# Roots of a layer norm moved from VectorE to GpSimd, and a new order for all pieces of a Fourier-mixing and feed-forward kernel

## The chip, the cores and the metric

The kernel runs on one core of a Trainium2 chip. The metric is the device time of one execution in microseconds (us), as the median of several runs; less is better. The core has five engines with a queue of instructions each: PE (TensorE, matmuls), DVE (VectorE), ACT (ScalarE), POOL (GpSimd) and SP (SyncE, which here only issues transfers). Each works through its own queue in order, and waits at an instruction until the semaphores that it needs are set.

## The reference

The input `x` has 2048 rows of 512 numbers. The first half mixes the normed rows by a discrete Fourier transform along both axes and keeps the real part; the second is a feed-forward block with SiLU. Both add their input back.

```python
def _layernorm(x, axis=-1, eps=1e-5):
    m = jnp.mean(x, axis=axis, keepdims=True)
    v = jnp.var(x, axis=axis, keepdims=True)
    return (x - m) / jnp.sqrt(v + eps)
...
    a = jnp.einsum("bsd,ed->bse", x, dft_hid_re)
    b = jnp.einsum("bsd,ed->bse", x, dft_hid_im)
    y = jnp.einsum("ts,bse->bte", dft_seq_re, a) - jnp.einsum("ts,bse->bte", dft_seq_im, b)
...
    h = jnp.einsum("bsd,df->bsf", x, w1)        # w1: 512 x 1792
    out = jnp.einsum("bsf,fd->bsd", _silu(h), w2)
...
    h = x + _A_ref(_layernorm(x, axis=-1), ...)
    h2 = h + _B_ref(_layernorm(h, axis=-1), B_w1, B_w2)
```

All is in 32-bit floats. The change concerns the second norm, that of `h`.

## The kernel before, in words

**The products.** Each matrix product is split into blocks of two by two, and seven block products (numbered 1 to 7 in the code) replace the eight. Each factor is split into a rounded part and its remainder (`ph` and `pl`, `gth` and `gtl`, `wah` and `wal`, ...): ACT writes the rounded part (`rounded`, L301), DVE the remainder (L305 or L307), and a product takes three matmuls, high by high, high by low and low by high (`three`, `mul_add`, L364). So each piece of data passes ACT and then DVE before PE can use it.

**The stages** run in this order on PE: `plain` and `fast` (the transform along the rows, tiles `raw` from `in_seq`, accumulated as `c` and `m`), `mix_fast(0)` (the transform along the columns, `y`, which gives `h` for one half of the 2048 positions, q = 0), then `fast` twice and `mix_fast(1)` for the other half, q = 1; then `up(0)` (first feed-forward product), `down(0)` (second), `up(1)` and `down(1)`. In `up`, a bank `y` holds one block product; ACT seeds a second bank `vx` from it (L1127), reads finished banks into tiles `g` with SiLU (L1113) or as a copy (L1116), and DVE adds a bank to `g` (L1119).

**The accumulating loads.** In `fast`, one of the operands of product 4 is made by a transfer: POOL issues a load that adds to a tile already in memory (`prep(4, jj)`, L783, `raw<-in_seq` on POOL). It can only be issued when product 6 no longer needs the tile (its remainder, L307, is the last reader), and must land before ACT and DVE can round it for product 4.

**The norm of h** is done by `norm_h`, once for each q and each half `tau`: four times. Rows of `h` lie along the partitions' direction here, so sums run over the partitions: `total` (L951 to L953) adds tiles on DVE and then reduces over all partitions on POOL (`partition_all_reduce`). The steps are: mean (`m`), centering (`hr`, L970), squares (`sq`, ACT, L974), variance (`v`), `row` (L980: POOL writes one row of sums to memory, `tk<-v`), `gather` (L985: POOL reads it back as 128 x 4, `rs<-tk`), `root` (L988 and `guess`) and `finish` (`steps`), both on DVE: they make 1/sqrt by an integer guess and three Newton steps, 12 instructions of 128 x 4; then POOL writes the result (L994, `tk<-rs`) and `spread` reads it to all partitions (L997, `v<-tk`), DVE scales `hr` (L1001) and POOL stores it (`nd<-hr`, L1006). `up` loads it later as `hn`.

**What sets the order.** Each piece (a function that issues a few instructions) gets a time when `program` builds its list: the time of the matmuls that need it, less a lead. A table `MOVED` adds a number of us to almost every one of these times, by the piece's number, and the pieces are issued in the order of the sums:

```python
    return sorted(((t + MOVED.get(n, 0.0), at, n, f) for t, at, n, f in events), key=lambda v: v[:3])
```

`fnet_ffn_kernel` ties the instructions of each engine to this order. The numbers mean nothing else: no time is waited for.

Of the kernel before, what the change touches and what calls it, by code (L numbers as in the profile page):

```python
# [10 lines left out]
I32 = mybir.dt.int32  # L11
# [37 lines left out]
    0: -293.31, 1: -238.02, 2: -236.08, 3: -179.9, 4: -165.03, 5: -165.94, 6: -230.19, 7: -165.91, 8: -166.37, 9:  # L49
    -169.09, 10: -87.55, 11: -75.38, 12: -79.62, 13: -88.41, 14: -92.69, 15: -95.8, 16: -82.48, 19: -265.67, 20:  # L50
    -161.2, 21: -158.27, 22: -323.002, 23: -165.782, 24: -160.652, 26: -268.028, 27: -160.838, 28: -143.038, 30:
    -169.334, 31: -135.774, 32: -99.584, 33: -268.444, 34: -162.004, 35: -86.794, 36: -89.044, 37: -319.344, 38:
    -134.664, 39: -53.134, 40: -18.294, 41: -135.054, 42: -110.964, 44: -173.98, 45: -89.04, 46: -19.29, 48:
    -180.186, 49: -98.766, 50: -24.876, 52: -185.652, 53: -171.502, 54: -73.442, 56: 0.292, 57: -19.018, 58: 0.252,
    59: -274.468, 60: -148.358, 61: -33.588, 62: 8.892, 63: -181.978, 64: -103.138, 65: -34.758, 66: -2.358, 67:
    -66.878, 68: -27.768, 69: -25.578, 71: -43.566, 72: -38.236, 73: -59.346, 74: -38.886, 75: 10.024, 76: 1.064,
    78: -16.394, 79: -14.734, 80: -26.784, 81: -5.694, 82: -0.564, 84: -41.482, 85: -36.432, 86: -157.702, 87:
    -22.612, 88: -7.752, 89: -7.192, 91: -2.708, 92: -3.74, 93: -2.72, 94: -64.5, 95: -32.87, 96: 1.73, 97: 0.63,
    98: -27.44, 99: -34.19, 100: -7.38, 101: 0.97, 102: -18.82, 103: -15.52, 104: -11.25, 106: -2.098, 107: -14.178,
    108: -61.718, 109: -48.848, 110: -158.978, 111: -50.148, 112: -26.248, 114: 1.066, 115: 2.704, 116: 7.464, 118:  # L60
    -9.124, 119: -1.244, 121: -6.812, 122: -8.972, 123: -6.6, 125: 1.36, 126: -14.5, 127: -11.28, 129: 4.452, 130:
    0.362, 131: 6.052, 132: -3.788, 133: -5.948, 135: -7.456, 136: -8.176, 138: 6.046, 139: -21.664, 140: -11.904,
    142: -1.932, 143: -0.232, 145: 1.25, 146: -25.88, 147: -6.3, 148: 21.31, 149: -4.7, 150: -20.4, 151: -8.98, 152:
    -7.15, 153: 28.75, 154: 25.81, 155: -12.71, 156: 17.2, 157: 14.33, 158: 24.01, 159: 24.3, 160: -25.07, 161:
    -19.07, 162: -1.94, 163: -9.48, 164: -10.03, 165: -0.79, 166: -3.22, 167: -4.24, 168: -0.47, 169: -1.31, 170:
    -20.28, 171: -13.2, 172: -9.02, 173: -7.06, 174: -8.33, 175: 7.5, 176: 2.08, 177: 4.54, 178: 4.16, 179: 7.35,
    180: -87.56, 181: -39.38, 182: -35.83, 183: -51.3, 184: -49.53, 185: -33.05, 186: -38.96, 187: -40.12, 188: -33,
    189: -7.63, 190: -7.07, 191: -7.39, 192: -28.2, 193: -21.42, 194: -12.55, 195: -45.58, 196: -38.52, 197: -25.77,
    198: -18.72, 199: -6.37, 200: 1.76, 201: -8.06, 202: -8.83, 203: 0.74, 204: -13.44, 205: -35.74, 206: -14.86,
    207: -15.13, 208: -14.61, 209: -14.99, 210: -11.05, 211: -13.19, 212: -1.42, 213: -6.67, 214: 2.44, 215: 3.39,  # L70
    216: 2.15, 217: 13.71, 218: 15.04, 219: -19.36, 220: -15.08, 221: -8.75, 222: -16.8, 223: -12.74, 224: -12.69,
    225: -2.55, 226: 1.87, 227: 7.08, 228: -24.27, 229: 4.79, 230: 6.22, 232: -11.018, 233: -2.838, 234: 4.432, 236:
    -5.006, 237: -3.076, 238: -0.206, 240: -7.874, 241: 1.516, 242: -0.314, 244: 2.218, 245: -10.572, 246: -7.142,
    247: 3.998, 249: 2.16, 250: 3.43, 251: 1.34, 253: 1.272, 254: 9.412, 255: 7.882, 257: -20.866, 258: -2.706, 259:
    1.564, 261: 8.456, 262: 3.496, 263: 4.736, 264: 5.326, 266: 1.238, 267: 4.798, 268: 3.258, 270: -3.49, 271: 2.1,
    272: 7.94, 274: 4.282, 275: 3.402, 276: 5.252, 278: 3.804, 279: 4.694, 280: 6.494, 281: -2.616, 282: -2.776,
    283: -1.126, 284: -6.436, 286: 2.026, 287: 5.116, 289: -8.752, 290: -0.782, 292: 7.54, 293: 5.47, 294: 6.35,
    295: 8.38, 296: 7.83, 297: 0.87, 299: 4.962, 300: 4.012, 301: 6.532, 303: -3.486, 304: 0.024, 306: 1.046, 307:
    -0.484, 309: 1.838, 310: 4.768, 311: 3.708, 312: 2.558, 313: 1.518, 314: -1.802, 316: 0.69, 317: 5.59, 318:
    2.19, 320: 3.402, 321: 5.322, 323: 4.884, 324: 4.194, 326: 4.326, 327: 4.666, 328: 6.196, 329: 5.956, 330:  # L80
    6.206, 331: -3.854, 333: 3.888, 334: 5.218, 335: 3.598, 336: 6.828, 338: -2.26, 339: 1.69, 341: -0.06, 342:
    -4.778, 343: -2.228, 345: 2.484, 346: 5.364, 347: 5.104, 348: 10.804, 350: 3.936, 351: -23.884, 352: -20.924,
    353: -3.474, 354: -1.064, 355: -3.958, 356: -1.394, 357: 1.542, 358: 4.454, 359: -1.334, 360: -4.352, 361:
    -1.014, 362: 0.566, 363: -7.054, 365: -0.542, 366: -0.194, 367: 0.208, 369: -1.59, 370: -0.702, 371: 2.89, 372:
    -1.892, 374: 3.672, 375: 3.862, 376: -7.108, 378: 5.504, 379: 11.454, 380: 0.624, 381: 3.244, 382: -7.318, 384:
    5.186, 385: 5.316, 386: -4.694, 388: 0.178, 389: 6.128, 390: 7.108, 391: 4.988, 392: -4.022, 394: -3.05, 395:
    0.01, 396: 0.91, 398: 2.112, 399: 5.002, 400: 4.232, 401: -3.148, 403: 3.004, 404: 7.374, 405: -13.516, 407:
    -2.874, 408: 0.456, 409: 6.836, 410: 4.696, 411: -1.684, 413: -2.082, 414: 2.008, 415: -4.502, 417: 4.08, 418:
    11.49, 419: 1.48, 420: -0.59, 421: 0.25, 423: -1.248, 424: -3.288, 425: -2.488, 427: 6.394, 428: 6.564, 429:
    16.874, 430: -13.816, 431: -15.286, 432: -16.006, 433: -16.926, 434: -18.866, 435: -13.776, 436: -14.006, 437:  # L90
    -14.416, 438: -11.876, 439: -2.636, 440: 5.724, 441: 4.534, 442: -2.046, 443: 4.424, 444: -32.796, 445: -23.056,
    446: -33.396, 447: -25.156, 448: -20.266, 449: -17.146, 450: -18.596, 451: -10.076, 452: -14.966, 453: -16.196,
    454: -8.346, 455: -8.386, 456: -15.576, 457: 7.224, 458: -31.606, 459: -1.696, 460: -0.956, 462: 11.206, 463:
    7.706, 464: 7.99, 466: -1.482, 467: -3.772, 468: 2.778, 470: 2.2, 471: 6.07, 472: 5.6, 474: 5.262, 475: -6.768,
    476: 7.382, 477: 5.232, 479: -3.576, 480: 4.644, 481: 2.494, 483: 1.896, 484: 1.986, 485: 7.656, 487: -32.282,
    488: -0.712, 489: -2.882, 491: 10.11, 492: 5.77, 493: 7.89, 494: 6.92, 496: 1.662, 497: 6.492, 498: 5.412, 500:
    3.054, 501: 2.056, 502: 2.074, 504: 13.106, 505: 6.506, 506: 4.726, 508: -0.03, 509: -0.312, 510: -2.412, 511:
    -11.742, 512: 0.03, 513: -1.16, 514: -12.122, 516: -2.98, 517: 0.14, 519: -2.788, 520: -4.408, 522: 1.934, 523:
    0.184, 524: -4.466, 525: -2.436, 526: -0.846, 527: -1.086, 529: 3.666, 530: 3.496, 531: -0.814, 533: -1.692,
    534: -1.132, 536: 3.25, 537: 3.27, 539: 7.492, 540: 5.312, 541: 0.362, 542: 2.642, 543: 8.322, 544: 1.364, 546:  # L100
    7.504, 547: 5.364, 548: 6.754, 550: -3.354, 551: 0.166, 553: 2.108, 554: 3.918, 556: 3.74, 557: 2.83, 558: 3.97,
    559: 2.9, 560: 2.21, 561: 1.07, 563: 2.202, 564: 2.302, 565: 2.142, 566: 8.252, 568: -5.946, 569: 0.184, 571:
    -0.01, 572: 6.046, 573: 4.706, 575: 7.928, 576: 4.098, 577: 1.978, 578: 5.368, 580: 16.1, 581: -43.508, 582:
    8.75, 583: 22.1, 584: 0.32, 585: 7.64, 586: 2.056, 587: 1.89, 589: -3.098, 590: -7.808, 591: -3.528, 593:
    -3.066, 594: -2.026, 595: 1.884, 597: 1.186, 598: -1.804, 599: -1.514, 601: 5.168, 602: 3.658, 603: 7.348, 604:
    7.838, 606: 9.74, 607: 4.81, 608: 5.2, 610: -46.978, 611: 9.892, 612: 7.782, 614: -4.116, 615: -2.096, 616:
    5.034, 618: 8.296, 619: 1.676, 620: 4.576, 621: 5.266, 623: -14.632, 624: 1.758, 625: 2.508, 627: 6.85, 628:
    4.44, 629: 5.41, 631: -3.658, 632: 1.672, 633: 3.992, 635: 3.514, 636: -6.306, 637: -5.556, 638: -26.046, 639:
    -27.206, 640: -24.446, 641: -25.296, 643: -9.124, 644: -6.024, 646: 2.478, 647: 1.388, 649: 1.76, 650: 3.11,
# [1330 lines left out]
```

## Time and profile before

| | us |
|---|---|
| median of 3 timed runs | 647.86 |
| the three runs | 647.58, 647.86, 649.74 |
| the profiled execution | 645.56 |
| its span, from the first to the last instruction | 643.8 |

In rows of the profile a time is counted from the start of the span. In a row of a timeline stand start, length, engine, line, operation, written tile `<-` read tiles, their shapes and a count `x2`; in brackets the idle time of the engine ahead of it and what ended it. In a row of groups stand the busy time and the mean in ns, then the idle time ahead of the instructions of the group. Rows with PEq, POOLq or SPq are those of an engine's sequencer or queue of transfers. Matmuls overlap: each row is longer than the time to the next one.

### The profile page before, as it was taken

The page shows a single profiled execution, that of the slowest core. Times are in us where ns is not written, and L with a number is a line of the kernel's source. Part 1 is how long each engine was busy: PE and PEld are TensorE (multiplying, and loading weights), DVE is VectorE, ACT ScalarE, POOL GpSimd, SP SyncE. Part 2 cuts the span into 40 slices and gives each one's busy share as a digit, 9 for nine tenths or more (in the row PEclk, how much of TensorE's full clock was granted, in tenths as well). Part 3 has the DMA queues.
Part 4 walks back from the last instruction along what each step waited for, and adds up shares of the span by engine and source line. Part 5 has one row for each costly group of instructions (what it writes and reads, how often), then busy time and mean ns, then how long its engine had stood idle before and what let it go on. Part 6 is the DMA issues. An engine that isn't in the chain of part 4 may idle for free. (4 is left out here: it accounts for less than half of the span.)

```text
span 643.8 us, 8291 instructions
## 1 busy us (share of the span) xinstructions
PE 631.3 (98%) x2892; PEld 543.9 (84%) x2892; DVE 562.2 (87%) x700; ACT 375.8 (58%) x484; POOL 110.1 (17%) x139
## 2 busy tenths in 40 slices
PE   9999999999999999999999999999999999999996
PEld 6888888888888888888888878877888888888885
DVE  7999999998978999999999999988989864479974
ACT  6898456765546545455855753779445555664700
POOL 0021111223103431310220027243010000000000
PEclk9999999999999999999999999999999999999999
DMA  9976899999999786999999899959998845278903
GB/s 317 369 184 147 261 358 377 302 322 358 330 306 350 242 263 154 367 361 331 333 352 396 281 295 373 382 207 328 362 369 287 297 147 177 82 261 309 344 33 131
DMA packets 59706, 184.22 MB, mean 286 GB/s; under 512 B 6800, under 2 KB 13840, under 8 KB 59664
## 3 DMA queue, kind: packets, MB, share of 16 engines
q1 hardware_dynamic: 43872, 127.03, 54.4%
q0 software_dynamic: 15504, 56.39, 29.1%
q8 instruction: 23, 0.38, 0.2%
q10 hardware_dynamic: 288, 0.26, 0.1%
q14 instruction: 19, 0.16, 0.1%
HBM read 139.34 MB, written 44.32 MB: 285 GB/s over the span
## 5 line engine op out<-in xcount | busy, mean ns | idle before, releaser
L301 ACT ACTIVATE ph<-raw 128x1024 fp32r<-128x1024 f32 x102 | 104.3, 1050 | 87.4 <-DMA raw<-in_seq 30.8
L364 PE MATMUL m<-ph,S 128*128 128x512 f32 x384 | 116.7, 379 | 0.0
L305 DVE TENSOR_TENSOR pl<-raw,ph 128x1024 fp32r<-128x1024 f32 x88 | 107.7, 1242 | 10.3 <-ACT ph L301 9.6
L364 PE MATMUL f<-gth,wf 128*128 128x512 f32 x322 | 98.1, 379 | 0.0
L364 PE MATMUL m<-ph,X 128*128 128x512 f32 x288 | 88.4, 379 | 0.0
L364 PEld LDWEIGHTS m<-ph,S 128*128 128x128 f32 x384 | 72.6, 189 | 10.2
L364 PE MATMUL m<-pl,S 128*128 128x512 f32 x192 | 72.9, 380 | 0.5 <-DVE pl L305 0.5
L364 PEld LDWEIGHTS f<-gth,wf 128*128 128x128 f32 x322 | 60.9, 189 | 8.8
L364 PE MATMUL y<-ph,hf 128*128 128x512 f32 x224 | 67.2, 379 | 0.3 <-DVE h L884 0.3
L364 PE MATMUL f<-gtl,wf 128*128 128x512 f32 x161 | 61.1, 380 | 0.0
L364 PEld LDWEIGHTS m<-ph,X 128*128 128x128 f32 x288 | 54.4, 189 | 7.6
L301 ACT ACTIVATE gth<-g 128x1024 fp32r<-128x1024 f32 x42 | 43.0, 1051 | 25.3 <-DVE g L1250 20.3
L364 PE MATMUL m<-pl,X 128*128 128x512 f32 x144 | 54.9, 381 | 0.2 <-DVE pl L305 0.2
L305 DVE TENSOR_TENSOR gtl<-g,gth 128x1024 fp32r<-128x1024 f32 x42 | 50.1, 1217 | 3.8 <-ACT gth L301 3.7
L364 PE MATMUL c<-ph,X 128*128 128x512 f32 x176 | 51.2, 381 | 0.5 <-DVE X L461 0.5
L364 PEld LDWEIGHTS y<-ph,hf 128*128 128x128 f32 x224 | 42.3, 189 | 6.6 <-issue 0.7
L769 DVE TENSOR_TENSOR raw<-raw,raw 128x1024 f32<-128x1024 f32 x36 | 45.8, 1274 | 2.1 <-DMA raw<-in_seq 1.7
L364 PE MATMUL y<-pl,hf 128*128 128x512 f32 x112 | 42.7, 381 | 1.2 <-DVE pl L305 1.2
L364 PEld LDWEIGHTS m<-pl,S 128*128 128x128 f32 x192 | 36.3, 189 | 6.0 <-DVE pl L305 0.9
L1119 DVE TENSOR_TENSOR g<-vx,g 128x512 f32<-128x512 f32 x28 | 19.3, 688 | 23.8 <-PE vx L364 12.0
L364 PEld LDWEIGHTS c<-ph,X 128*128 128x128 f32 x176 | 33.1, 189 | 6.0 <-DVE X L461 0.9
L364 PEld LDWEIGHTS f<-gtl,wf 128*128 128x128 f32 x161 | 30.4, 189 | 4.6 <-DVE gtl L305 0.3
(360 smaller groups left out, 1269.1 us busy)
## 6 DMA issues: line engine op xcount, KB each, us to landing
raw<-in_seq SPq DMA_DIRECT2D x84, 512.0 KB, 6.2
hf<-fd SPq DMA_DIRECT2D x28, 512.0 KB, 6.5
wf<-wd SPq DMA_DIRECT2D x28, 512.0 KB, 6.7
wf<-wd SPq DMA_DIRECT2D x28, 384.0 KB, 4.5
sf<-sd SPq DMA_DIRECT2D x18, 512.0 KB, 5.9
raw<-in_seq POOLq DMA_DIRECT2D x16, 512.0 KB, 6.8
fd<-hf POOLq DMA_DIRECT2D x14, 512.0 KB, 6.5
w<-in_ffn SPq DMA_DIRECT2D x23, 256.0 KB, 6.0
```

Source lines behind the costliest of these rows:

```text
L301: nc.scalar.activation(hi, src, AF.Copy, scale=sign)
L305: nc.vector.tensor_tensor(lo, src, hi, op=ALU.subtract)
L364: nc.tensor.matmul(acc, w, turned(m), **flags)
L769: nc.vector.tensor_tensor(o, a, b, op=ALU.subtract)
L1119: nc.vector.tensor_tensor(g[q, f][:, tau, :], src, g[q, f][:, tau, :], op=ALU.add)
```

## The change

**Roots on POOL.** `guess` and `steps` are gone. `root` now issues three instructions on GpSimd, one of them a power with exponent −0.5 (a tile `power` filled with it); `finish` issues four, one Newton step, and the transfer as before. The power and the reduction over partitions belong to different libraries of GpSimd, so a library change (a row `ISA` without tiles) stands ahead of the first root after a reduction, and of the first reduction after a root. A single power on one column is issued early, as a single reduction was before.

```diff
 MOVED = {
-    0: -293.31, 1: -238.02, 2: -236.08, 3: -179.9, 4: -165.03, 5: -165.94, 6: -230.19, 7: -165.91, 8: -166.37, 9:
...
+    power = keep.tile([P, 4], F32, name="power")
...
-    def guess(v, t, r, b):
-
-        nc.vector.tensor_scalar(r.bitcast(I32), v.bitcast(I32), -0.5, float(0x5F3759DF), op0=ALU.mult, op1=ALU.add)
-        newton(v, t, r, b)
-
-    def steps(v, t, r, b):
-        newton(v, t, b, r)
-        newton(v, t, r, b)
...
         def root():
-            nc.vector.tensor_scalar(ln["w"][0], ln["w"][0], 1.0 / D, EPS, op0=ALU.mult, op1=ALU.add)
-            nc.vector.tensor_scalar(ln["w"][1], ln["w"][0], -0.5, None, op0=ALU.mult)
-            guess(*ln["w"])
+            v, t, r, _ = ln["w"]
+            nc.gpsimd.tensor_scalar(v, v, 1.0 / D, EPS, op0=ALU.mult, op1=ALU.add)
+            nc.gpsimd.tensor_tensor(r, v, power, op=ALU.pow)
+            nc.gpsimd.tensor_scalar(t, v, -0.5, None, op0=ALU.mult)
 
         def finish():
-            steps(*ln["w"])
-            nc.gpsimd.dma_start(token[1].rearrange("(p j) -> p j", j=4), ln.pop("w")[3])
+            v, t, r, b = ln["w"]
+            nc.gpsimd.tensor_tensor(v, r, r, op=ALU.mult)
+            nc.gpsimd.tensor_tensor(v, v, t, op=ALU.mult)
+            nc.gpsimd.tensor_scalar(v, v, 1.5, None, op0=ALU.add)
+            nc.gpsimd.tensor_tensor(b, v, r, op=ALU.mult)
+            nc.gpsimd.dma_start(token[1].rearrange("(p j) -> p j", j=4), b)
...
+    nc.gpsimd.memset(power, -0.5)
     at(100, lambda: nc.scalar.activation(spare[:, :1], spare[:, 1:], AF.Silu))
+    at(105, lambda: nc.gpsimd.tensor_tensor(spare[:, :1], spare[:, 1:], power[:, :1], op=ALU.pow))
     at(110, lambda: nc.gpsimd.partition_all_reduce(spare[:, :1], spare[:, 1:], channels=P, reduce_op=REDUCE_ADD))
```

**A new order.** Nearly all entries of `MOVED` (1207 of 1208) have other numbers. PE's instructions keep their sequence; on DVE, ACT, POOL and SP pieces change places, by a few places mostly. DVE has 48 instructions fewer, POOL 37 rows more. Three places show it.

First, POOL during `fast(0, 1)`, the first transform stage for q = 1 (about 213 to 250 us of the span), from the first variance's row of sums to the transfers behind its root. `tk` and `rs` are the tokens of the norm, `m` the sums of the next mean, `raw` the accumulating loads, `cd` a store. Before:

```order
L980 DMA tk_82<-v_1972 16x1x32
L783 DMA raw_1855<-in_seq 128x1024
L985 DMA rs_2062<-tk_82 128x4
L953 ISA m_2097<-m_2097 128x512
L505 DMA cd_73<-c_2106 128x1024
L783 DMA raw_2009<-in_seq 128x1024
L994 DMA tk_83<-rs_2062 128x4
L783 DMA raw_2116<-in_seq 128x1024
L997 DMA v_1972<-tk_83 128x512
```

In the same place after the change:

```order
L976 DMA rs_2128<-tk_83 128x4
L944 ISA m_2130<-m_2130 128x512
L980 ISA
L980 TENSOR_SCALAR rs_2128<-rs_2128 128x4
L981 TENSOR_TENSOR rs_2128<-rs_2128,power 128x4
L982 TENSOR_SCALAR rs_2128<-rs_2128 128x4
L774 DMA raw_1981<-in_seq 128x1024
L986 TENSOR_TENSOR rs_2128<-rs_2128 128x4
L987 TENSOR_TENSOR rs_2128<-rs_2128 128x4
L988 TENSOR_SCALAR rs_2128<-rs_2128 128x4
L989 TENSOR_TENSOR rs_2128<-rs_2128 128x4
L990 DMA tk_84<-rs_2128 128x4
```

The second of the accumulating loads (`raw_2009` before, `raw_1981` now) now stands behind the library change and the first three instructions of the root, and the third one behind the rest of it and the spread.

Second, DVE near the end of `up(0)` (about 437 to 443 us). `g` are the results of the first product, `b` and `gtl` remainders for the second, `rs` the root. Before, from just behind the first of the two additions to the tile `g_3833` to the second:

```order
L1238 TENSOR_TENSOR b_3897<-g_3663,b_3897 128x512
L988 TENSOR_SCALAR rs_3873<-rs_3873 128x4
L989 TENSOR_SCALAR rs_3873<-rs_3873 128x4
L333 TENSOR_SCALAR rs_3873<-rs_3873 128x4
L345 TENSOR_TENSOR rs_3873<-rs_3873 128x4
L346 TENSOR_TENSOR rs_3873<-rs_3873 128x4
L347 SCALAR_TENSOR_TENSOR rs_3873<-rs_3873 128x4
L1238 TENSOR_TENSOR b_3891<-g_3441,b_3891 128x512
L1250 TENSOR_TENSOR g_3663<-g_3663 128x512
L1238 TENSOR_TENSOR b_3964<-g_3515,b_3964 128x512
L305 TENSOR_TENSOR gtl<-g_3442,gth 128x1024
L1119 TENSOR_TENSOR g_3833<-vx_3822,g_3833 128x512
```

After, from the first addition to the same tile (now `g_3821`) to the second:

```order
L1115 TENSOR_TENSOR g_3821<-vx_3809,g_3821 128x512
L942 TENSOR_TENSOR v_3908<-sq_3874,sq_3868 128x1024
L943 TENSOR_TENSOR v_3908<-v_3908 128x512
L1234 TENSOR_TENSOR b_3818<-g_3439,b_3818 128x512
L304 TENSOR_TENSOR gtl<-g_3440,gth 128x1024
L1234 TENSOR_TENSOR b_3899<-g_3731,b_3899 128x512
L1115 TENSOR_TENSOR g_3821<-vx_3809,g_3821 128x512
```

The root is gone from between them, three other rows moved behind, and the two rows of the last variance, which stood ahead of the first addition, came in.

Third, ACT in the middle of `up(0)` (about 417 to 421 us), from the seeding of one bank `vx` to the release of the one before (`g<-vx`). `wah` and `wS5h` are rounded weights, `sq` squares of the norm. Before:

```order
L1127 ACTIVATE vx_3734<-y_3719 128x512
L1086 ACTIVATE wah_3748<-w_3631 128x768
L974 ACTIVATE sq_3762<-hr_3644 128x1024
L1113 ACTIVATE g_3663<-y_3646 128x512
L301 ACTIVATE wS5h<-ws_3757 128x1024
L1116 ACTIVATE g_3746<-y_3719 128x512
L1113 ACTIVATE g_3663<-vx_3656 128x512
```

After:

```order
L1123 ACTIVATE vx_3720<-y_3713 128x512
L965 ACTIVATE sq_3736<-hr_3680 128x1024
L965 ACTIVATE sq_3744<-hr_3689 128x1024
L1082 ACTIVATE wah_3755<-w_3645 128x768
L1109 ACTIVATE g_3440<-g_3440 128x512
L1109 ACTIVATE g_3655<-y_3631 128x512
L1112 ACTIVATE g_3732<-y_3713 128x512
L300 ACTIVATE wS5h<-ws_3748 128x1024
L1109 ACTIVATE g_3655<-vx_3638 128x512
```

A second square and one more `g` row stand between the seed and the release.

More of the change, by code (lines that the diff above doesn't have):

```diff
@@ L10 @@
 F32R = mybir.dt.float32r
-I32 = mybir.dt.int32
 AF = mybir.ActivationFunctionType
```

283 rows, old and new, of the table MOVED are left out of this document.

## The prediction

> **What bounds the kernel now.** The first part of the page shows whose work fills the span.
>
> ```profile
> span 643.8 us, 8291 instructions
> PE 631.3 (98%) x2892; PEld 543.9 (84%) x2892; DVE 562.2 (87%) x700; ACT 375.8 (58%) x484; POOL 110.1 (17%) x139
> ```
>
> TensorE is busy for 98%, so only what makes TensorE wait can be won. Busy matmuls overlap, so a lost microsecond shows better in the weight loads (PEld), one for each matmul. Next I read the busy times by stage. The columns are the stretch, its length, then busy time and count of PE, PEld, DVE, ACT and POOL, the granted clock, DMA share and GB/s.
>
> ```profile
> 5.80:84.30 78.50, 78.03 (x362) 67.79 (x361) 75.35 (x136) 63.30 (x92) 6.94 (x9) 1.00 0.84 263
> ...
> 157.00:194.70 37.70, 36.77 (x169) 31.59 (x168) 29.87 (x26) 18.24 (x19) 4.44 (x4) 1.00 0.99 332
> 194.70:268.00 73.30, 72.63 (x334) 62.68 (x333) 68.70 (x67) 39.48 (x42) 25.70 (x22) 1.00 0.84 265
> 268.00:341.20 73.20, 73.20 (x340) 64.09 (x340) 69.22 (x84) 44.88 (x51) 12.62 (x21) 1.00 1.02 350
> 341.20:378.30 37.10, 36.57 (x170) 31.71 (x169) 34.91 (x38) 22.86 (x25) 3.72 (x5) 1.00 0.96 323
> 378.30:450.30 72.00, 68.74 (x309) 57.11 (x308) 66.04 (x87) 46.70 (x75) 33.30 (x39) 1.00 0.89 319
> ...
> 638.30:643.80 5.50, 0.02 (x1) 0.00 (x0) 0.42 (x1) 0.38 (x1) 0.00 (x0) 0.71 0.52 186
> ```
>
> The stretch from 268.0 to 341.2 runs without a gap: 64.09 of 73.20, or 0.875 of its length, is weight loading. By that rate 57.11 us of loads need 65.3 us, and the stretch from 378.3 to 450.3 took 72.0: 6.7 us are lost there. In the same way 1.0, 1.6, 1.7 and 0.9 us are lost in the other four stretches shown. So about 12 us of the span are waits inside it, and more than half lie in one stage, the first product of the feed-forward part (`up`, q = 0). The 5.8 us ahead of the first stretch and the 5.5 us of the last are the start and the last output, which the change leaves as they are but for a few exchanged rows. The clock is 1.00 wherever TensorE works, so no term comes from it.
>
> The largest single wait of that stage, from the timeline of PE, then of ACT, then of DVE:
>
> ```profile
> 446.95 0.38 PE L364 MATMUL y<-T3h,wS6l 128*128 128x512 f32 x1
> 448.76 0.48 PE L364 MATMUL vx<-T4h,wah 128*128 128x512 f32 x1 [1.43 <-ACT g L1113]
> ```
> ```profile
> 443.69 0.60 ACT L1113 ACTIVATE g<-vx 128x512 f32<-128x512 f32 x1 [1.58 <-DVE g L1119]
> ...
> 448.11 0.59 ACT L1113 ACTIVATE g<-vx 128x512 f32<-128x512 f32 x1
> ```
> ```profile
> 438.70 0.55 DVE L988 TENSOR_SCALAR rs<-rs 128x4 f32<-128x4 f32 x1
> ...
> 439.95 0.16 DVE L347 SCALAR_TENSOR_TENSOR rs<-rs 128x4 f32<-128x4 f32 x1
> ...
> 442.97 0.68 DVE L1119 TENSOR_TENSOR g<-vx,g 128x512 f32<-128x512 f32 x1
> ```
>
> Matmuls start 0.22 us apart when nothing is awaited, so 448.76 − 446.95 − 0.22 = 1.6 us are lost. This group waits for a bank that ACT releases at 448.70; ACT had stood still for 1.58 us until DVE's addition of 442.97; and DVE had spent 438.70 to 440.11 on `root`. From 443.69 on ACT has no idle, so what it lost there it hands on.
>
> **The change part by part.**
>
> *Roots off DVE.* There are four roots, each with 12 small operations on DVE. Their groups:
>
> ```profile
> L988 DVE TENSOR_SCALAR rs<-rs x4: 161/356/2207, 229.1 to 459.5; 128x4 f32<-128x4 f32 x4
> L989 DVE TENSOR_SCALAR rs<-rs x4: 169/170/171, 231.3 to 459.7; 128x4 f32<-128x4 f32 x4
> ```
> ```profile
> 229.08 2.21 DVE L988 TENSOR_SCALAR rs<-rs 128x4 f32<-128x4 f32 x1
> ```
>
> All but the first operation of a root take about 0.16 us with a pitch of 0.2, so a root costs DVE 2.3 us, and 9 to 11 us go in all with the 2.21 of 229.08. That one fell into a reduction on POOL (228.20 for 4.06 us, below). I don't count that 2 us as won: reductions stay, and hold up another DVE row. What counts is the 1.41 us ahead of 442.97. Without it ACT starts 1.41 us sooner, and of the 1.6 us 0.2 are left. The new DVE order (second place shown above) also has five rows where eleven stood between the two additions to the same tile, so ACT's 1.58 us of idle can go altogether. I take −1.5 us, bounds −1.6 and 0 (if ACT is late for another reason).
>
> *Roots on POOL.* Per root there are seven small operations and a library change; and the reductions that follow change it back, seven changes in all where there was one. The trace has no such elementwise operation on POOL. It has one library change, ahead of the reduction of L1400:
>
> ```profile
> 144.13 0.86 POOL L783 DMA_DIRECT2D raw<-in_seq  x1 [5.80 <-DVE pl L307]
> 144.88 3.61 POOL L1400 PARTITION_ALL_REDUCE spare<-spare  x1
> 149.84 1.12 POOL L862 DMA_DIRECT2D fd<-hf  x2 [1.34 <-ACT ph L301]
> ```
>
> The next row starts 4.96 us after the reduction began, so the change and a reduction of one element cost at most 5.0 us; at least nothing. I take 3.6 us for a change, the duration of this row, since one element is hardly reduced for long, and 0.2 us for an operation, as on DVE. Whom does it hold up? The first root stands in POOL's queue ahead of the accumulating load `raw` that TensorE needs at the step of 247.43:
>
> ```profile
> 228.20 4.06 POOL L953 PARTITION_ALL_REDUCE m<-m  x1 [6.29 <-issue]
> 232.14 0.56 POOL L505 DMA_DIRECT2D cd<-c  x1
> 232.69 0.92 POOL L783 DMA_DIRECT2D raw<-in_seq  x1
> ```
> ```profile
> raw<-in_seq POOLq DMA_DIRECT2D x16, 512.0 KB, 6.8
> ```
> ```profile
> L301 ACT ACTIVATE ph<-raw 128x1024 fp32r<-128x1024 f32 x102 | 104.3, 1050 | 87.4 <-DMA raw<-in_seq 30.8
> ...
> L305 DVE TENSOR_TENSOR pl<-raw,ph 128x1024 fp32r<-128x1024 f32 x88 | 107.7, 1242 | 10.3 <-ACT ph L301 9.6
> ```
> ```profile
> 247.43 0.38 PE L364 MATMUL m<-ph,X 128*128 128x512 f32 x1
> 247.64 0.38 PE L364 MATMUL m<-pl,X 128*128 128x512 f32 x1
> ```
>
> If the reduction ends at 232.3 as before, the load is issued at 232.3 + 3.6 + 0.6 = 236.5, lands 6.8 later at 243.3, is rounded by ACT (1.05) and DVE (1.24), and is ready at 245.6. TensorE wants the remainder at 247.64. So 2.0 us are left, and a change of up to 5.6 us is free. The later changes stand ahead of an operation that waits for a transfer or for DVE anyway, and run meanwhile. And before, POOL waited for DVE's roots, in the waits of POOL (us in total, times, longest):
>
> ```profile
> POOL tk L994 <- DVE rs L347: 34.5, 4, 18.3
> ```
>
> The longest of these, 18.3 us, belongs to q = 1, so there the finished roots come sooner, not later. I take 0 for POOL, bounds −0.5 (POOL waits less for DVE) and +4.4 (a change of 10 us, twice the most that the row allows). The Trainium skill, "GPSIMD Engine Reference", section "Instruction dispatch", says that the first call into a freshly loaded library pays about 6 us that no instruction shows. The rows above leave at most 5.0 for it, so the trace bears the page out only in part. With 6 us the load would be 0.4 us late, and the sum higher by that.
>
> *The new order.* TensorE's own list keeps its sequence, so the work is the same and only waits move. Of the 12 us, 12 − 1.6 remain outside the wait at 448.76, in many shorter ones. A part of them comes from the reductions:
>
> ```profile
> 257.29 4.13 POOL L953 PARTITION_ALL_REDUCE v<-v  x1 [4.33 <-DVE v L952]
> ```
> ```profile
> 258.25 5.53 DVE L305 TENSOR_TENSOR pl<-raw,ph 128x1024 fp32r<-128x1024 f32 x3
> ```
> ```profile
> 263.83 0.48 PE L364 MATMUL m<-pl,S 128*128 128x512 f32 x1 [0.49 <-DVE pl L305]
> ```
>
> Three such operations take 3.7 us by the mean above, so these lost about 1.8 us during the reduction, and TensorE waited for the result. The reductions stay, so I count on a change of −0.5 us from waits outside the stage, with bounds −3 and +3: the trace of before can't show how a new order meets them.
>
> *Room for late transfers.* The profiled execution took 645.56 us, 1.8 more than its span. The three timed ones took 647.58, 647.86 and 649.74. The same list of matmuls took 2.0 to 4.2 us longer at a clock that the profile shows full, so I read the difference as more waiting. If transfers that land later cause it, an order with two us of room takes a part of it away. I take −0.8 us of the median's 2.3, bounds −2.3 and 0.
>
> Sum against the profiled execution, without the last part: 645.56 − 1.5 + 0 − 0.5 = 643.6. Set on the median, with a new stall of 0.5 for 1200 moved entries that can't all fall well: 647.86 − 1.5 − 0.5 − 0.8 + 0.5 = **645.6 us**. A measurement of this kernel can tell about 0.3%, or 1.9 us, from no change, so this is just beyond: faster by 0.35%.
>
> **The rivals.**
>
> *The waits move on (within 0.3%).* ACT and DVE have little slack in the stage from 378.3 to 450.3: DVE is busy 66.0 of 72.0. If the freed 1.4 us is taken up by the next late bank, and room for late transfers costs room elsewhere, only 0.3 to 1 us of gain is left: about 647.2. For it: the reductions and their DVE stalls stay. Against it: the largest wait has a traced cause that the change removes.
>
> *POOL's queue holds the loads (slower).* If a library change takes 10 us, the load above is ready at 252.0, 4.4 us late, and each later change has less cover. It decides from 5.6 us on. With the other gains kept this gives 645.6 + 4.4 = 650.0. Against it stands the 5.0 us bound; for it, that this bound is from one change at an idle moment.
>
> *ACT's order is worse in the same stage (slower).* A bank is released late at another place too:
>
> ```profile
> 416.73 0.58 ACT L1127 ACTIVATE vx<-y 128x512 f32<-128x512 f32 x1 [0.91 <-PE vx L364]
> ...
> 417.96 1.04 ACT L974 ACTIVATE sq<-hr 128x1024 f32<-128x1024 f32 x1
> ...
> 420.81 0.60 ACT L1113 ACTIVATE g<-vx 128x512 f32<-128x512 f32 x1
> ```
> ```profile
> 421.47 0.48 PE L364 MATMUL vx<-T4h,wah 128*128 128x512 f32 x1 [0.88 <-ACT g L1113]
> ```
>
> In the new list (third place shown above) a second square and a further `g` row stand between this seed and this release: 1.04 + 0.60 = 1.6 us later if ACT is as full as here. With the 0.5 us of new stalls, and no gain elsewhere, that gives 647.86 + 1.6 + 0.5 = 650.0.
>
> **How the numbers follow.** The forecast (faster) gets 0.50: one traced wait goes, and two further terms point down. The moved waits get 0.31. POOL's queue gets 0.12 and ACT's order 0.07, together 0.19 slower. The range takes in the larger order gain (its bound of −3 in place of −0.5 gives 643.1) as 643.0, and upward the moved waits and the first part of the slower cases, as far as 649.8. About 0.2 is left outside.
>
> **What would show it.** Right: no wait of PE above 1 us between 445 and 450; DVE busy time down by about 10 us; POOL's `raw` loads of L774 issued within 5 us of the end of the reduction ahead; timed runs closer to the profiled one. Wrong: a PE wait for `pl` near 247 with a POOL row of several us ahead of it (library), or again 6 us lost from 378 to 450 (moved waits). A time over 650 or under 643 would mean that a cost or a gain is at work that this trace doesn't hold.

## The result, and the profile after

The changed kernel takes 674.48 us (median of 673.06, 674.48 and 674.77), the kernel before beside it on the same chip 647.72 us: a ratio of 1.0406, interval 1.0365 to 1.0448. It is 27 us slower; the forecast was 2 us faster, and its range ended at 649.8. (A fourth run, slow at a granted clock of 0.75, took 831.93 us and is left out here and below.) The profiled execution took 673.06 us.

The first part of the page after:

```profile
span 671.3 us, 8266 instructions
PE 639.6 (95%) x2892; PEld 547.1 (82%) x2892; DVE 559.9 (83%) x652; ACT 375.9 (56%) x484; POOL 124.0 (18%) x169
```

DVE has its 48 instructions fewer, but is busy only 2.3 us less (562.2 before); POOL has 14 us more. TensorE does the same work at 95% in place of 98%. The busy times by stage, at the matmuls where a stage begins and ends (the columns are those of the prediction's stretches: length, PE, PEld, DVE, ACT, POOL, granted clock, DMA share, GB/s):

```profile
195.00:276.60 81.60, 75.39 (x338) 64.66 (x337) 70.32 (x56) 38.88 (x41) 30.72 (x30) 0.96 0.77 241
276.60:353.79 77.19, 74.39 (x338) 63.09 (x337) 66.05 (x70) 43.97 (x51) 15.78 (x29) 1.00 0.97 331
390.19:464.69 74.50, 66.25 (x296) 56.33 (x294) 63.02 (x76) 44.21 (x70) 30.25 (x34) 0.98 0.70 243
464.69:537.90 73.21, 66.48 (x296) 56.46 (x295) 56.80 (x65) 35.18 (x40) 17.17 (x27) 0.98 0.86 310
```

These four stretches hold the loss. The list of matmuls is the same as before, the lengths are not: PE is idle for 6.2, 2.8, 8.3 and 6.7 us of them. In three of them the clock is no longer 1.00. Since both kernels run the same list of matmuls, I compare the times between the same matmuls: from here on "a stage loses x us" means that against the profiled execution of before. That one ran 2 us under its median, so a loss of a microsecond or two can be noise: the first stage of the table loses 0.9 to 2.9 us in every run below, whatever was changed.

| stage | before, us | after loses |
|---|---|---|
| `plain`, `fast(1, 0)` | 151.2 | 1.5 |
| `mix_fast(0)` | 37.7 | −1.4 |
| `fast(0, 1)` | 74.0 | 7.6 |
| `fast(1, 1)` | 72.5 | 4.7 |
| `mix_fast(1)` | 37.1 | −0.7 |
| `up(0)` | 67.5 | 7.0 |
| `down(0)` | 65.3 | 8.0 |
| `up(1)`, `down(1)` | 126.7 | 1.4 |

**First place, 253 us.** POOL after, the stretch whose order the section on the change shows:

```profile
231.45 3.18 POOL L944 PARTITION_ALL_REDUCE m<-m  x1
243.13 1.87 POOL L980 TENSOR_SCALAR rs<-rs 128x4 f32<-128x4 f32 x1 [8.50 <-issue]
245.08 1.06 POOL L981 TENSOR_TENSOR rs<-rs,power 128x4 f32<-128x4 f32 x1
246.13 0.26 POOL L982 TENSOR_SCALAR rs<-rs 128x4 f32<-128x4 f32 x1
246.34 1.05 POOL L774 DMA_DIRECT2D raw<-in_seq  x1
```

The reduction ends at 234.6. Then POOL stands for 8.50 us, and the bracket names no engine and no transfer, only `issue`: that is the library change. The three operations of the root follow with 3.2 us, and only then the load is issued: at 246.34, where it was 232.69 before. ACT and PE wait for it:

```profile
252.08 1.06 ACT L300 ACTIVATE ph<-raw 128x1024 fp32r<-128x1024 f32 x1 [10.60 <-DMA raw<-in_seq]
```
```profile
253.19 0.79 PE L355 MATMUL m<-ph,X 128*128 128x512 f32 x1 [5.74 <-ACT ph L300]
254.45 0.79 PE L355 MATMUL m<-pl,X 128*128 128x512 f32 x1 [0.47 <-DVE pl L304]
...
257.60 0.81 PE L355 MATMUL m<-ph,X 128*128 128x512 f32 x2
258.25 0.38 PE L355 MATMUL m<-pl,X 128*128 128x512 f32 x1
```

The group of all four such operations says it in one row: of the 26.5 us that POOL is idle ahead of L980, `issue` has 26.4. Three of the four stand behind a change; the last two roots follow each other without one.

```profile
L980 POOL TENSOR_SCALAR rs<-rs 128x4 f32<-128x4 f32 x4 | 7.6, 1910 | 26.5 <-issue 26.4
```

**Second place, 490 to 503 us.** The chain that ended last, followed through `down(0)`:

```profile
466.20 5.05 DMA rs<-tk
471.25 5.75 issue
477.00 5.40 POOL rs L980
482.41 0.07 issue
482.48 1.06 POOL rs L981
483.54 0.21 POOL rs L982
483.75 5.03 DMA sd<-wS5h
...
489.82 1.05 ACT gth L300
```

The store `sd<-wS5h` has nothing to do with the norm. Its data was complete at 440.8 us, 43 us earlier, but it stands behind the root in POOL's queue; its memory comes free late, ACT writes `gth` late, and PE waits several times for the products `f`. Two of PE's waits in this stretch (us in all, times, longest):

```profile
PE f L355 <- ACT p L1268: 3.5, 2, 2.7
PE f L355 <- DVE gtl L304: 2.0, 2, 1.2
```

**Third place, 415 us.** No library change makes this wait: run 7 below has none, and waits here too. DVE, ACT and PE:

```profile
406.77 4.34 DVE L1045 TENSOR_TENSOR ws<-w 128x256 f32<-128x256 f32 x1
...
413.28 0.68 DVE L1115 TENSOR_TENSOR g<-vx,g 128x512 f32<-128x512 f32 x1
```
```profile
414.00 0.60 ACT L1109 ACTIVATE g<-vx 128x512 f32<-128x512 f32 x1 [7.27 <-DVE g L1115]
414.50 0.59 ACT L1123 ACTIVATE vx<-y 128x512 f32<-128x512 f32 x1
```
```profile
415.14 0.80 PE L355 MATMUL y<-T6h,wS2h 128*128 128x512 f32 x1 [5.15 <-ACT vx L1123]
```

A row that takes 0.42 us elsewhere takes 4.34 us here, while a reduction runs on POOL (from 408.64 for 3.18 us). The addition to `g` stands behind it and six further rows; ACT's SiLU read of the same bank now stands behind the addition, and the seed of the next bank behind that. Before, the SiLU read came ahead of the addition and of the sums `ws`, so DVE's hold did not reach ACT.

### The profile page after: what moved, and what is told of

Read it like the earlier page. It is cut to its first block, busy times and chain, and to the rows that moved or that the text cites. A ratio compares the mean times of both kernels' runs of the same rounds, so it can differ in the third digit from the quotient of the medians.

```text
span 671.3 us, 8266 instructions
## 1 busy us (share of the span) xinstructions
PE 639.6 (95%) x2892; PEld 547.1 (82%) x2892; DVE 559.9 (83%) x652; ACT 375.9 (56%) x484; POOL 124.0 (18%) x169
## 5 line engine op out<-in xcount | busy, mean ns | idle before, releaser
L304 DVE TENSOR_TENSOR pl<-raw,ph 128x1024 fp32r<-128x1024 f32 x88 | 113.2, 1309 | 20.6 <-ACT ph L300 14.1
L355 PE MATMUL f<-gth,wf 128*128 128x512 f32 x322 | 100.1, 385 | 4.7 <-ACT p L1268 3.5
L355 PE MATMUL m<-ph,X 128*128 128x512 f32 x288 | 90.1, 385 | 6.2 <-ACT ph L300 6.2
L304 DVE TENSOR_TENSOR gtl<-g,gth 128x1024 fp32r<-128x1024 f32 x42 | 52.6, 1270 | 12.3 <-ACT gth L300 12.3
L760 DVE TENSOR_TENSOR raw<-raw,raw 128x1024 f32<-128x1024 f32 x36 | 43.8, 1219 | 0.3
```

Of the source, the lines that this page charges most:

```text
L304: nc.vector.tensor_tensor(lo, src, hi, op=ALU.subtract)
L355: nc.tensor.matmul(acc, w, turned(m), **flags)
L760: nc.vector.tensor_tensor(o, a, b, op=ALU.subtract)
```

## The experiments

Theory at the start: POOL's library changes hold up the transfers queued behind them. Rival: the order itself. The runs of before beside them had medians of 648.12 (first four), 648.46 (fifth to eighth), 647.88 (ninth to twelfth) and 647.98 us (the last two).

**1. The order alone.** After, with the roots of before:

```diff
-            nc.gpsimd.tensor_scalar(v, v, 1.0 / D, EPS, op0=ALU.mult, op1=ALU.add)
-            nc.gpsimd.tensor_tensor(r, v, power, op=ALU.pow)
...
+            nc.vector.tensor_scalar(ln["w"][0], ln["w"][0], 1.0 / D, EPS, op0=ALU.mult, op1=ALU.add)
+            nc.vector.tensor_scalar(ln["w"][1], ln["w"][0], -0.5, None, op0=ALU.mult)
+            guess(*ln["w"])
```

> The kernel after, with its new order, but with the roots back on DVE as the 12 small operations of before. By the theory that the library changes of POOL hold up the transfers queued behind them, the waits at 253 us (9 us), in the second transform stage (4.7 us) and at 490 to 507 us (8 to 10 us) go, and what is left are the waits of the order in the stage from 378 us on (7 us): 650 to 656 us. By the rival that the new order is what costs, nearly all of the 27 us stay: 668 to 676 us. By the forecast's own rival, that the order's gains only need the roots off POOL, it is below 648 us.

Measured: 661.87 us, ratio 1.0211 (1.0168 to 1.0254). It lies between the two expectations: about half of the excess stays without any root on POOL. In its `up(0)` 7.3 us are lost, as after. In `fast(0, 1)` and `fast(1, 1)` 3.7 us each are lost, the first because the new order puts the root right behind its gather, and DVE waits there with its queue:

```profile
DVE rs L988 <- DMA rs<-tk: 5.1, 2, 3.8
```

**2. The roots alone.** After's code with before's `MOVED`.

> The kernel after, with its roots on POOL, but with the order of before for all pieces. Library theory: two or three of the four roots still stand ahead of loads or stores, so 658 to 670 us, with idle of 7 to 10 us on POOL ahead of L980 or its like. Order theory: within 2 us of the kernel before, 646 to 650 us.

Measured: 669.92 us, 1.0330 (1.0292 to 1.0369). So the order is not the only cause. But 9.4 us of the excess are lost in `mix_fast(0)`, where after loses nothing: before's order puts the early reduction ahead of the early power, and each pays a change (9.16 and 7.74 us of idle). Behind the first stand the stores `fd` that this stage reads: they are issued at 156.78, in before at 149.84.

**3. The changes alone.** Before, with one power of a column that nothing uses:

```diff
             guess(*ln["w"])
+            nc.gpsimd.tensor_tensor(spare[:, :1], spare[:, 1:], power[:, :1], op=ALU.pow)
```

> The kernel before, with its roots on DVE and its order, and one power of a single column more on POOL at each of the four places of the root (and one early), that nothing uses: library changes without any work moved. Library theory: nearly as slow as the roots on POOL in the order of before, 655 to 668 us. Rival that the roots' own operations on POOL, or that what waits for them, cost the time: 647 to 650 us.

Measured: 660.75 us, 1.0182 (1.0137 to 1.0226). Library changes alone cost time, though no work was moved. Here too 8.5 us lie in `mix_fast(0)`; run 11 takes that away.

**4. Transfers ahead of the roots.** After, with the first two roots moved back in POOL's queue and the stores `sd` moved forward:

```diff
-    438: -9.856, 439: 1.044, 440: -1.626, 452: -14.966, 453: -16.196, 454: -16.176, 996: 31.909, 1019: 38.594
+    438: -1.991, 439: 1.409, 440: -1.59, 452: -2.851, 453: -5.35, 454: -8.349, 996: 13.497, 1019: 22.284
```

> The kernel after, with three of its four roots moved in POOL's queue behind transfers that nothing of the root needs: the accumulating load of 246 us ahead of the first root, the next one ahead of its second half, the two stores cd ahead of the second root, the stores sd of wS5 and wS6 ahead of the last two. Library theory (the queue behind the change is what costs): the waits at 253 us, in the second transform stage and at 490 us shrink, 12 to 17 us come back, 656 to 663 us. Rival that a late root costs by what waits for the norm itself, or the order: no more than 4 us come back, 670 to 676 us.

Measured: 689.05 us, 1.0630 (1.0593 to 1.0668): 14.6 us more than after, where 12 to 17 less were expected. The mend made it worse. DVE's waits, then DVE and POOL near the last of them:

```profile
DVE hr L997 <- DMA v<-tk: 38.1, 3, 12.8
```
```profile
493.85 1.22 DVE L304 TENSOR_TENSOR gtl<-g,gth 128x1024 fp32r<-128x1024 f32 x1
...
504.95 0.69 DVE L1246 TENSOR_TENSOR g<-g 128x512 f32<-128x512 f32 x1
518.39 2.36 DVE L997 TENSOR_TENSOR hr<-hr,v 128x1024 f32<-128x1024 f32 x2 [12.75 <-DMA v<-tk]
```
```profile
493.86 11.84 POOL L980 TENSOR_SCALAR rs<-rs 128x4 f32<-128x4 f32 x1 [10.58 <-issue]
```

Three times DVE stands for over 12 us at the scaling of `hr`, which waits for the root, with every row behind it that TensorE needs; after has no such wait. So a change costs in either place: what stands behind it in POOL's queue is late, or the norm is late and holds DVE's queue. The last row shows that the change is not all of this: the root's first small operation took 11.84 us (the last section says beside what).

**5. The roots alone, the early power first.** Run 2 with the sequence of after at that one place:

```diff
-    1533: 47.148, 1534: 40.89
+    1533: 45.89, 1534: 81.66
```

> The roots on POOL in the order of before, as in the run with the roots alone, but with the early power ahead of the early reduction, as in the kernel after: so the two early changes no longer stand ahead of the stores that the stage at 157 to 195 us reads. If the excess of the run with the roots alone is made of two parts, the 9.4 us of that stage (early changes) and 12 us behind the four roots, it is now 658 to 662 us. If the early changes only moved a wait that comes anyway, it stays at 667 to 671 us.

Measured: 659.92 us, 1.0173 (1.0142 to 1.0204). The split of run 2 holds: 10 us were the early changes, the four roots on POOL cost 11.5 us in the old order.

**6. No roots in the old order.** The arithmetic of `root` and `finish` left out:

```diff
         def root():
+            pass
...
+            nc.gpsimd.dma_start(token[1].rearrange("(p j) -> p j", j=4), ln.pop("w")[0])
```

> The kernel before, with the arithmetic of the four roots left out: the sums of squares are sent on in place of the roots (the second norm is not computed). It shows what roots that cost nothing anywhere would be worth in the order of before. The forecast's first step, a wait of 1.6 us at 448.76 us that DVE's root causes: 645.5 to 646.7 us, and no wait of PE above 0.5 us there. Rival, the waits move on: 647.3 to 648.3 us.

Measured: 645.55 us, 0.9962 (0.9944 to 0.9980). Free roots would be worth 2.9 us, so the first step had a real prize. The profiled execution took 648.77 us, 3 us over the median, so I read only one wait from it: the one that the forecast's first step named, at 448.76 in before, shrinks from 1.43 to 0.66 us, a little over the expected 0.5.

```profile
452.82 0.48 PE L364 MATMUL vx<-T4h,wah 128*128 128x512 f32 x1 [0.66 <-ACT g L1110]
```

**7. No roots in the new order.** The same edit in run 1's kernel.

> The order of after with the arithmetic of the roots left out in the same way: the order alone, with no root on either engine. If the 13.7 us of the run with the order alone come from DVE's roots standing in places that were laid out for POOL's, it is 648 to 652 us. If they come from where the order puts the reductions and the readers of banks, it is 657 to 662 us, with the wait of 5 us near 409 us and that of 3 us near 445 us still there.

Measured: 649.13 us, 1.0012 (0.9998 to 1.0027). The time fits the first expectation, the waits fit the second: both waits in `up(0)` are there and the stage loses 6.8 us, while `mix_fast(0)`, `fast(0, 1)`, `mix_fast(1)` and `down(0)` win 5.5 together. So the order has real gains and one bad stage; my second number had left the gains out.

```profile
PE y L364 <- ACT vx L1124: 4.9, 1, 4.9
PE y L364 <- ACT g L1113: 2.6, 1, 2.6
```

**8. The SiLU read ahead.** After, with two pieces of `up(0)` moved:

```diff
-    914: 4.784, 919: 1.576
+    914: 2.504, 919: -0.184
```

> The kernel after with two pieces moved ahead in the first product of the feed-forward part: the copy and the addition that release one bank, and the SiLU read that releases the other, stand ahead of DVE's sums of a weight (the rows that the reductions hold up for 4.3 us), as they do before. Theory that the wait of 5.2 us at 415 us is made by this order: it goes, 667 to 670 us. Rival that the reduction's hold passes on to whatever row stands there: 672 to 676 us.

Measured: 668.04 us, 1.0306 (1.0277 to 1.0335): 6.4 us back. (In the kernel before, too, the addition comes behind the sums; I had written otherwise. Only the SiLU read stands ahead.) The wait of 5.2 us is gone, so the third place is made by the order of two pieces against a row that the reductions hold. But `up(0)` itself gets back only 3.8 us in the profiled execution: 2.4 us of waiting for an ACT copy stand at 415.26 in its place.

**9. The new order mended, roots on DVE.** Run 1 with the edit of run 8, `983: 5.39` and `960: 9.478` for the second read, and the roots later (`438: -4.596`, `439: -7.086`, `453: -17.456`, `795: 31.759`, `796: 29.261`, `809: 35.109`).

> The order of after with the roots on DVE, and three mends: the pieces of the run with the SiLU read ahead; a SiLU read of the same kind, before it the product that writes the other half of its bank (the wait of 2.6 us near 445 us); and DVE's roots moved behind rows that need not wait for the gather, with their second half right behind the first. Theory that the order's gains of 3 us in the stages up to 380 us are real and its losses are these three places: 640 to 645 us, faster than before by 0.5 to 1.2%. Rival that mended waits come back at the next late row: 647 to 652 us.

Measured: 651.30 us, 1.0064 (1.0042 to 1.0086). The rival is right: `up(0)` is mended to 0.5 us of loss, `fast(0, 1)` to 0.4, but `down(0)` still loses 3.4. No version that computes everything beat the kernel before.

**10. The same without roots.**

> The order of after with the two mends for the SiLU reads, and the arithmetic of the roots left out (the sums are sent on in their place, the second norm is not computed). The run without roots in this order lost 6.8 us in the first product of the feed-forward part against before: if the two reads are the whole of it, 640 to 643 us; if only the first, 643 to 646 us.

Measured: 644.27 us, 0.9950 (0.9927 to 0.9973). A wait of 2.0 us for an ACT copy was left in `up(0)`. Against run 6 the new order, mended, takes 1.3 us less; the two intervals overlap, so that gain is not shown.

**11. The changes alone, the early power first.** Run 3 with the edit of run 5.

> The order of before with its roots on DVE, and one power of a single column on POOL at each root's place that nothing uses, now with the early power ahead of the early reduction. The library changes alone, without any root moved. With the roots on POOL the same order took 659.9 us. If the change itself (7 to 9 us of POOL's queue, with stores and loads behind it) is the whole price, 657 to 661 us; if half of it is that the root's own small operations on POOL are late or slow, 651 to 655 us.

Measured: 652.94 us, 1.0091 (1.0057 to 1.0125). Changes alone cost 5.1 of the 11.5 us of run 5 in this order. The difference lies in `fast(1, 1)`, 0.0 against 5.2 us: with the root on POOL the stores `cd` are issued at 293.18, with only the change at 283.44. The unused power awaits nothing and starts at 282.12; the root awaits its gather and starts at 286.73, then takes 5.4 us for its seven operations.

**12. No reductions.** After, with no library change left:

```diff
-        nc.gpsimd.partition_all_reduce(t[:, 1, :], t[:, 0, :], channels=P, reduce_op=REDUCE_ADD)
+        nc.gpsimd.tensor_tensor(t[:, 1, :], t[:, 0, :], t[:, 0, :], op=ALU.add)
```

> The kernel after with the reduction over the partitions left out: a plain addition on POOL stands in its place (so the sums of the second norm stay those of one partition), and no library change is left, while all operations of the roots stay on POOL. If the changes make the price of the roots, the gaps of 7 to 10 us ahead of L980 are gone and the time falls by over 15 us, to 646 to 657 us, the waits of the order in the first product of the feed-forward part among what is left. If the roots' operations themselves make it, 664 to 672 us.

Measured: 644.53 us, 0.9945 (0.9920 to 0.9971): 30 us less than after, below what was expected, and faster than before. All operations of the roots are still on POOL, and the first now follows at once:

```profile
230.13 1.09 POOL L944 TENSOR_TENSOR m<-m 128x512 f32<-128x512 f32 x1
231.48 0.88 POOL L980 TENSOR_SCALAR rs<-rs 128x4 f32<-128x4 f32 x1 [0.26 <-DMA rs<-tk]
```

But this run also took away the reductions' length, 3 to 4 us of POOL and their hold on DVE. The last two runs part these.

**13 and 14. Reductions of one column**, in before (control) and in after:

```diff
-        nc.gpsimd.partition_all_reduce(t[:, 1, :], t[:, 0, :], channels=P, reduce_op=REDUCE_ADD)
+        nc.gpsimd.partition_all_reduce(t[:, 1, :1], t[:, 0, :1], channels=P, reduce_op=REDUCE_ADD)
```

> The kernel before with the reductions over the partitions cut to one column of 512 (the other columns of the sums keep what the addition left there, so the second norm is not computed): the length of the eight reductions and their hold on DVE go, no library changes are there in either. If the holds are what makes the run without reductions fast, 641 to 645 us. If they cost little, 645 to 648 us.

Measured: 646.07 us, 0.9968 (0.9943 to 0.9993).

> The kernel after with the reductions cut to one column in the same way: the library changes and the roots on POOL stay as they are, the length of the reductions goes. If the changes are the price (the run without reductions took 644.5 us), nearly all of the excess over that run is still there: 660 to 670 us. If the reductions' length and hold were, it is 645 to 652 us.

Measured: 660.24 us, 1.0188 (1.0158 to 1.0218). POOL at the first root:

```profile
230.42 1.44 POOL L944 PARTITION_ALL_REDUCE m<-m  x1
240.40 0.72 POOL L980 TENSOR_SCALAR rs<-rs 128x4 f32<-128x4 f32 x1 [8.54 <-issue]
```

The gap is there, undiminished, behind a reduction of one column. Against run 12, run 14 has 15.7 us more, and by stage they lie where the roots are: 6.3 in `fast(0, 1)`, 2.1 in `fast(1, 1)`, 8.6 in `down(0)`. That is the price of the library changes with what follows from them. Not all of it is the length of a change: in `down(0)` the root's first operation starts at 463.13 and takes 8.11 us, in run 12 it starts at 452.03 and takes 0.23. The change moved it beside rows of DVE that hold it (last section); no run parts the two. The time lies at the low end of what was expected, but "nearly all of the excess" was too high: the other 14.2 us of after come with the length of the reductions, which costs before only 1.9 us. After minus run 14 is 5.9 us in `up(0)` (the third place), 2.8 and 1.6 in the two `fast` stages, where a longer reduction starts the change later.

## Why the prediction was wrong

The times of the two parts side by side, in us (the cells come from several series, beside which before took 647.7 to 648.5):

| | no roots | roots on DVE | roots on POOL |
|---|---|---|---|
| order of before | 645.55 | 648.46 | 659.92 |
| order of after | 649.13 | 661.87 | 674.48 |

*Roots off DVE, −1.5.* The sign was right, and it is worth 2.9 us where nothing takes the roots' place. The wait at 448.76 fell by half without the roots (run 6); in the new order it is gone, with the roots on POOL as well as on DVE (run 1), so the order removes it too. What I set aside, "I don't count that 2 us as won: reductions stay, and hold up another DVE row", was the right thought with no price. The other rows are now of a group that TensorE reads (in `m`, its waits for `pl` rose from 0.7 to 3.0 us, in part behind the late load of the first place):

```profile
L304 DVE TENSOR_TENSOR pl<-raw,ph 128x1024 fp32r<-128x1024 f32 x88 | 113.2, 1309 | 20.6 <-ACT ph L300 14.1
```

Before, the same 88 rows took 107.7 us. Of the roughly 10 us that left DVE, 5.5 came back in these rows.

*Roots on POOL, 0.* **This is the step that failed**: "so the change and a reduction of one element cost at most 5.0 us". The row behind that bound is the first use of the only library in its program, not a change from one to another. The same row in run 1, also a program with reductions as its only library:

```profile
187.24 0.65 POOL L1400 PARTITION_ALL_REDUCE spare<-spare  x1
```

0.65 us, with nothing idle ahead: the first reduction of that program pays nothing. So the 3.61 us of the row in before need not hold a change at all; what lengthened it, no run shows. In run 3, whose program has both libraries, the same early reduction, again the first use, does pay:

```profile
155.51 0.96 POOL L1404 PARTITION_ALL_REDUCE spare<-spare  x1 [8.67 <-DVE wS1l L305]
```

The bracket names what came last; in run 2 the same place has 9.16 us with `issue`. Why a first use costs nothing in one program and that much in the other stays open.

I took 3.6 us for a change; it measured 8.50 us at the first root, where the forecast itself said that all above 5.6 us is late. The first three operations of the root measured 3.2 us in place of 0.6. The prediction had cited the Trainium skill, "GPSIMD Engine Reference", section "Instruction dispatch", for about 6 us that no instruction shows, and let the false bound override it. The rows agree with the page that no instruction shows it. Most changes of the runs put it at 6.0 us (run 5, ahead of the reduction at 402.58) to 9.2 us (run 2); the longer ones, up to 11.7 us, await a transfer or DVE too, but for one of 11.37 us in run 4.

The second half of the step failed as well: "The later changes stand ahead of an operation that waits for a transfer or for DVE anyway, and run meanwhile." A change did not run wholly under the awaited transfer: in the chain of the second place 5.75 us are left between the landing of the gather and the operation. And I looked at the operation behind the change and not at the transfers behind that one. The stores `cd` and `sd` are such, and run 4 shows that putting them first makes the norm late instead.

*The new order, −0.5.* Against run 6, run 7 has 3.6 us more, just outside the bounds of 3. The stages around `mix_fast` won, `up(0)` lost 6.8. The rival "ACT's order is worse in the same stage" had the stage and the kind of wait, but not the place, and 1.6 us in place of 5.2 and 2.6. The matmul at 421.47 that it named does not wait in after; those that wait stand at 398.62 and 432.64 in before. I had compared the order with the trace where before already waited. The wait of 5.2 stands where the reductions hold DVE; the one of 2.6 is there without any reduction too (run 12), so it is the order's own. With the roots on DVE this order costs 13.4 us, though no library change is left: the table shows that the order and the place of the roots are not separate terms that can be added.

*Room for late transfers, −0.8.* Not settled. Without roots the runs in the new order lie 2.6 us apart (647.78 to 650.39, ten runs), in the old 4.7 (644.06 to 648.77, twelve runs), but the median of the new order is higher.

*The rivals.* "POOL's queue holds the loads" was the right mechanism, with a chance of 0.12. For a change of 10 us it took 0.6 us for the root's first three operations, which took 3.2, and it charged the first root alone: 650.0. With reductions of one column, the changes and what follows from them are 15.7 us, in three places.

*What would show it wrong* was named rightly: a PE wait near 247 with POOL rows of several us ahead is the first place, and 7.0 us more are lost in `up(0)`. One sign of being right held as well: no wait of PE above 1 us stands where before had the one at 448.76.

## What to carry to other kernels

An operation that moves to another engine takes its place in that engine's queue, and that queue may issue transfers that others live on: price what stands behind it, transfer by transfer, and what waits for its result. A bound taken from a row holds only if the row contains the thing bounded; the first use of a library need not show what a later change costs. When an order is written out by hand, look in the new one for the rows that a long shared hold will fall on, and for readers of a bank that come behind them.

## What the hardware showed beyond that

*Idle of TensorE is paid twice.* In the first place above, after 5.74 us of waiting, matmuls start 0.43 us apart up to 257.6 and 0.22 from 258.25 on. That is some 2 us on top of the wait. The granted clock is 0.50 from 251.2 to 258.0, and 0.96 over the whole stage. The Trainium skill, "TensorE: Matmul & The Clock Gate", section "What's actually happening", has the array at half its clock after an idle window of about 3.4 us until a busy one of that length; the pitch here agrees, but the slow matmuls lasted about 4.8 us, longer than that. It is not in the prediction's sums.

*A small operation on POOL waits for a pause of DVE.* In run 4 the 128x4 operation at 493.86 took 11.84 us, to 505.70: DVE's rows follow each other without a gap from before it to 505.64. After has it twice, 1.87 us at 243.13 and 5.39 us at 477.00, and run 14 with 8.11 us; without such neighbours the same operation takes 0.19 us (283.01 in after). The Trainium skill, "SBUF — State Buffer", section "Who interferes with whom", says that a DVE instruction with two inputs and a GpSimd instruction that reads exclude each other for a whole instruction. Here POOL's one operation did not get in between two of DVE's, but waited out fifteen of them.

*Which library comes first matters.* With both in the program, an early power before the early reduction pays one change of 6.8 us in a quiet place (run 5); the other way round both pay, 9.16 and 7.74 us (run 2), and the time is 10 us longer.
